# Another order table for a kernel planned by hand: which engine copies and squares, and where a zero-product stands

## The chip, the cores and the metric

The kernel runs on one core of a Trainium2 chip. The metric is the time of one execution in microseconds (us), the median of several runs. A core has a matrix engine (TensorE; PE in the profile, with its weight loads as PEld), a vector engine (VectorE, DVE), a scalar engine (ScalarE, ACT), GpSimd (POOL) and SyncE (SP), which here only issues transfers. Each engine works through its own list of instructions in order; semaphores make one wait for another. SBUF is the working memory, PSUM the eight banks into which PE writes.

## The reference, cut to what matters

```python
# q, k, v: (8, 8, 576, 64); w_in: (512, 1024); w_out: (1024, 512)
kv  = einsum('bhsd,bhse->bhde', k, v)
out = einsum('bhsd,bhde->bhse', q, kv)
x   = out / sqrt(mean(out * out, -1) + 1e-6) * g_norm      # then (4608, 512)
h   = x @ w_in
sm  = softmax(h, -1)
s   = h * sm
ln  = (s - mean(s)) / sqrt(var(s) + 1e-6) * g_ln
y   = ln @ w_out                                            # (4608, 512) float32
```

## The kernel before, in words

There are eight batches, b = 0 to 7. The kernel works in nine chunks c of 512 tokens: chunks 0 to 7 take eight of every nine tokens of a batch, and chunk 8 collects the ninth ones of all batches (`q_last`). Heads come in two halves (`hf`), d_ff in eight slices of 128 (`f`), the tokens of a chunk in four groups (`m`).

Nothing is scheduled by a planner at run time. The source registers named pieces of work, and the text `ORDER` lists all 907 of them; the pieces are emitted in that order, and so each engine's list of instructions is the part of the table that is its own. A suffix (`:act`, `:dve`, `:pool`) sets another engine than the piece's first one. `ROOMS` gives, digit by digit, the buffer of each tile when it is first used (for a PSUM tile one of the eight banks); a piece that takes a buffer waits until the users of the tile that was in it are done. `WARM` says how many products of zeros each `warm` piece has; they only keep PE running.

The pieces, with their lines:

- `k`, `v`, `q`, `q_last`, `w_in`, `w_out` (L322, L338, L343, L348): loads issued by POOL, which convert to bf16 where the tile is bf16. `wide.k` and `wide.v` (L328) bring heads 4 to 7 of batch 0 as float32 on SP's queue, and the pieces `k.0.1` and `v.0.1` copy them to bf16 (L229).
- `kv_mm` (L375): k times v on PE; `kv.b.x.part` (L229): its copies from PSUM.
- `qT_mm` (L427) and its copy `qT.c.hf` (L229): q turned by PE for chunks 0 to 3. For chunks 4 to 8 `qT.c` is one turning transfer on SP's queue (L435).
- `o_mm` (L448): q times kv. `sq` (L233): its squares; `oa` (L460): two halves of them added; `s_mm` (L465): their mean; `ln`, `ex` (L472, L476; chunk 0 by L482): one over the root; `x` (L489): the normalized input of h.
- `h.c.f.part` (L532), in two parts of two matmuls for chunks 0 to 2 and whole afterwards; `exp` (L539) to the tile e; `u` (L543): h times e; `usq` (L233 on ScalarE, L235 on GpSimd): squares of u; `es` (L551, GpSimd): sums of two slices of e.
- `ua`, `usqa`, `esa` (L575): folds of u, its squares and the sums of e on VectorE, for chunks 1 to 8 (esa for 5 to 8).
- `sums` (L594), `turn` (L601), `stats` (L606 to L611), `rstd` (L615, L617): the statistics of the layer norm, `w_mean` (L632) and `w_center` (L638): w_out less its mean.
- `out` (L651; the last group of chunk 8 in two halves, L659), `ob` (L239 on ScalarE, L241 on VectorE): scaled results; `store` (L679, L675).

Three rules tie engines together beside the data. After a fold or an added square on VectorE, the next listed piece of GpSimd waits for it; a turning transfer waits for the last load but one that was issued before it; and a load listed after a turning transfer waits for that:

```python
if engine == "pool":
    self.after(ins, self.adds)
    self.adds.clear()
if name[0] in ("ua", "usqa", "esa", "oa") and engine == "dve":
    self.adds.append(ins)
elif name[0] in ("k", "v", "q", "q_last", "w_in", "w_out") and engine == "pool":
    self.after(ins, self.turns)
...
elif name[0] == "qT" and engine == "sp":
    self.after(ins, self.loads[-2:-1])
    self.turns.append(ins)
```

Of the kernel before, what the change touches and what calls it, by code (L numbers as in the profile page):

```python
# [25 lines left out]
kv.1.0.0.0 kv.1.0.1.1 kv.1.0.1.0 qT_mm.1.0 ex.0.0 q.2.0 qT.1.0:act x.0.0.0 x.0.0.1 warm.5 o_mm.1.0 sq.1.0.0 warm.6
h.0.6.0 h.0.3.0 k.2.0 sq.1.0.1 x.0.1.0 table h.0.0.0 oa.1.0 x.0.1.1 s_mm.1.0 h.0.2.0 h.0.7.0 h.0.2.1 ln.1.0 v.2.0
ex.1.0 h.0.6.1 x.1.0.1 exp.0.6 q.3.0 h.0.3.1 exp.0.2 x.1.0.0 h.0.7.1 h.0.1.0 exp.0.7 u.0.6 v.3.0 qT_mm.1.1 h.0.0.1
exp.0.3 h.0.1.1 u.0.2 usq.0.6 h.1.2.0 exp.0.0 qT.1.1 kv_mm.1.1.1 exp.0.1 kv_mm.1.1.0 k.3.0 kv.1.1.0.1 h.0.4.0 h.0.4.1
u.0.1 kv.1.1.2.1:act kv.1.1.0.0:act es.0.0 kv.1.1.1.0:act kv.1.1.2.0:act kv.1.1.1.1 u.0.3 o_mm.1.1 exp.0.4 h.0.5.0  # L30
# [5 lines left out]
w_center.7 exp.1.4 h.1.5.0 w_center.6 kv.2.1.0:act kv.2.0.0:act h.1.5.1 kv.2.0.2:act kv.2.1.1 kv.2.0.1:act es.1.1  # L36
u.1.4 out.0.2.2 kv.2.1.2:act exp.1.5 o_mm.2.0 u.1.3 o_mm.2.1 sq.2.0.1 out.0.2.3 usq.1.1 u.1.2 qT_mm.3.0 sq.2.0.0 u.1.5
out.0.0.0 sq.2.1.1 oa.2.0 out.0.0.1 sq.2.1.0 qT.3.0 s_mm.2.0 usq.1.5 out.0.0.2 ln.2.0 qT_mm.3.1 oa.2.1:pool ex.2.0
h.1.6.0 qT.3.1 out.0.0.3 usq.1.2:act x.2.0.0 x.2.0.1 h.1.6.1 s_mm.2.1 exp.1.6 sums.0 usq.1.7 ln.2.1 u.1.6 ex.2.1
kv_mm.3.0 es.1.2 turn.0 stats.0 out.0.3.0 kv.3.1.0:act x.2.1.0 x.2.1.1 usq.1.0:act out.0.3.1 usq.1.4 usq.1.3 h.2.6.0  # L40
# [10 lines left out]
exp.3.6 x.4.1.1 h.3.1.0 exp.3.5 q.6.0 usq.2.2:act h.3.4.0 usq.3.3 ob.1.2:act usq.2.1:act usq.2.3:act exp.3.4 es.3.1
u.3.7 u.3.5 store.1.2 h.4.6.0 u.3.6 k.6.0 u.3.4 h.4.7.0 exp.3.1 out.1.1.0 out.1.1.1 exp.4.7 usq.3.2:act h.3.0.0
usqa.2.0 usqa.2.1 exp.4.6 ob.1.1:act u.4.7 kv_mm.5.0 usq.3.5 exp.3.0 u.3.1 sums.2 kv.5.0.1:act es.3.3 h.4.5.0
usq.4.7:act u.4.6 kv.5.0.0:act kv.5.1.2:act h.4.4.0 q.7.0 kv.5.0.2 kv.5.1.1:act u.3.0 kv.5.1.0:act exp.4.5 o_mm.5.1
es.3.0 turn.2 o_mm.5.0 sq.5.1.0 out.2.3.0 stats.2 u.4.5 sq.5.1.1 out.2.3.1 exp.4.4 oa.5.1 ua.3.0 rstd.2 s_mm.5.1
out.2.0.0 ln.5.1 u.4.4 sq.5.0.0 out.2.0.1 sq.5.0.1 ua.3.1 h.4.0.0 ob.2.3:act oa.5.0 ob.2.0 ex.5.1 s_mm.5.0 es.4.2
store.2.3 h.4.2.0 ln.5.0 x.5.1.0 h.4.3.0 store.1.1 usq.3.6 exp.4.2 x.5.1.1 ex.5.0 usq.3.4:act kv_mm.6.0 u.4.2 usq.3.0
qT.6 out.2.1.0 out.2.2.0 kv.6.1.0 kv.6.0.0 es.4.3 kv.6.1.2 x.5.0.0 out.2.2.1 usq.3.7:act qT.7 x.5.0.1 exp.4.3
usq.3.1:act h.4.1.0 es.3.2 kv.6.1.1:act u.4.3 usq.4.5:act kv.6.0.1 ob.2.2:act store.1.0 usqa.3.0 h.5.3.0 exp.4.1
kv.6.0.2:act h.5.6.0 store.2.0 exp.5.3 exp.4.0 usqa.3.1 u.4.1 h.5.7.0 es.4.0 es.4.1 usq.4.6:act u.4.0 out.2.1.1  # L60
exp.5.6 u.5.3 exp.5.7 o_mm.6.0 ob.2.1 o_mm.6.1 sq.6.0.0 sums.3 u.5.6 store.2.1 out.3.0.0 sq.6.0.1 u.5.7 usq.4.2:act
oa.6.0 out.3.0.1 sq.6.1.1 ua.4.0 sq.6.1.0 s_mm.6.0 out.3.3.0 ln.6.0 oa.6.1 turn.3 out.3.3.1 ex.6.0 v.7.0 stats.3
q_last.3 s_mm.6.1 x.6.0.0 h.5.0.0 ln.6.1 k.7.0 x.6.0.1 h.5.2.0 ex.6.1 q_last.1 exp.5.0 x.6.1.0 h.5.5.0 q_last.7
exp.5.2 u.5.0 h.5.4.0 rstd.3 es.5.1 x.6.1.1 usq.4.4:act out.3.1.0 ob.3.0 exp.5.4 es.5.3 h.6.6.0 usq.4.3:act ob.3.3
usq.4.0:act u.5.4 h.6.3.0 exp.5.5 ua.4.1 h.5.1.0 usq.4.1:act u.5.5 q_last.0 exp.6.6 out.3.1.1 u.5.2 q_last.4
# [670 lines left out]
```

## Time and profile before

| | |
|---|---|
| median of three runs | 177.41 us (176.84 to 177.65) |
| span of the profiled execution, first to last instruction | 175.8 us |
| what lies around it, against that median | 1.6 us |
| PE busy | 164.2 us |
| ScalarE busy | 152.1 us |
| VectorE busy | 145.5 us |
| GpSimd busy | 99.8 us |
| granted clock of PE | 1.000 |

A row of the timeline gives the start in us, the duration in us, engine, line, operation, output and input tiles with their shape, how many instructions were merged (x), and in brackets the idle time of the engine before it and what ended it. Durations of neighbours overlap a little, because one instruction ends its writes while the next begins; the interval from start to start is the price in a full queue. Rows of groups give the mean in ns after the sum. SPq and POOLq are the queues' own times.

### The profile page before, as it was taken

To read this page: it belongs to the slowest core of one execution; us is meant where nothing else is said; L and a number is where in the kernel's file an instruction comes from. 1 tells how busy PE (TensorE), PEld (TensorE's weight loads), DVE (VectorE), ACT (ScalarE), POOL (GpSimd) and SP (SyncE) were. 2 spreads that over 40 slices of the span, in tenths; PEclk is the share of its full clock that TensorE was granted. 3 is DMA by queue.
4 is the path that set the end of the run, shared out by engine and by line. 5 is a ranking of instruction groups with operands and counts; after the bars stand their busy time and mean duration, and the time that the engine had idled before them with its cause. 6 is when DMAs were issued, how large, how long until landed. Compare 5 with 4: busy or idle time off the path is not lost.

```text
span 175.8 us, 4843 instructions
## 1 busy us (share of the span) xinstructions
PE 164.2 (93%) x1913; PEld 80.3 (46%) x1938; DVE 145.5 (83%) x317; ACT 152.1 (86%) x273; POOL 99.8 (57%) x108
## 2 busy tenths in 40 slices
...
GB/s 179 218 203 214 206 275 373 209 208 208 208 210 210 218 210 129 127 206 235 205 183 259 150 52 193 156 73 93 195 206 105 5 118 126 2 60 93 196 213 159
DMA packets 34623, 30.27 MB, mean 172 GB/s; under 512 B 16288, under 2 KB 28328, under 8 KB 34600
## 3 DMA queue, kind: packets, MB, share of 16 engines
...
q8 instruction: 15, 0.25, 0.6%
q14 instruction: 8, 0.07, 0.1%
HBM read 32.51 MB, written 9.44 MB: 239 GB/s over the span
## 4 chain that ended last, share of the span: by engine, by line
PE 75%; DVE 10%; ACT 5%; DMA 5%; issue 2%; POOL 1%; POOLq 0%; DVEq 0%; ACTq 0%
PE h_ps L532 31%; PE out_ps L651 30%; DMA k_sb<-in_k_dram 5%; PE kv_ps L375 4%; PE o_ps L448 3%; DVE u_sb L543 3%; PE sum_ps L594 3%; PE s_ps L465 3%; DVE x_sb L489 2%; DVE w_out_sb L638 2%; ACT osq_sb L233 2%; DVE osq_sb L460 1%; PE out_ps L659 1%; ACT e_sb L539 1%; ACT kvd L229 1%
## 5 line engine op out<-in xcount | busy, mean ns | idle before, releaser
L532 PE MATMUL h_ps<-x_sb,w_in_sb 128*128 128x512 bf16 x280 | 68.0, 379 | 0.5
L651 PE MATMUL out_ps<-w_out_sb,u_sb 128*128 128x512 bf16 x266 | 65.2, 379 | 0.7 <-issue 0.3
L551 POOL TENSOR_TENSOR es_sb<-e_sb 128x512 bf16<-128x512 f32 x36 | 45.4, 1279 | 33.5 <-ACT e_sb L539 13.0
L539 ACT ACTIVATE e_sb<-h_ps,zero_t 128x512 f32<-128x512 f32 x72 | 46.2, 690 | 2.3 <-PE h_ps L532 1.7
L543 DVE TENSOR_TENSOR u_sb<-h_ps,e_sb 128x512 bf16<-128x512 f32 x72 | 46.6, 684 | 1.3 <-ACT e_sb L539 1.0
L532 PEld LDWEIGHTS <-w_in_sb 128*128 128x128 bf16 x288 | 27.3, 98 | 32.5 <-issue 1.3
L651 PEld LDWEIGHTS <-u_sb 128*128 128x128 bf16 x280 | 26.4, 98 | 31.6 <-issue 1.0
L233 ACT ACTIVATE usq_sb<-u_sb,zero_t 128x512 bf16<-128x512 bf16 x49 | 33.6, 718 | 0.0
L489 DVE SCALAR_TENSOR_TENSOR x_sb<-o_ps,g_sb,rst_sb 128x256 bf16<-128x256 f32 x72 | 30.2, 478 | 3.1 <-ACT rst_sb L476 2.5
L235 POOL TENSOR_TENSOR usq_sb<-u_sb 128x512 bf16<-128x512 bf16 x23 | 23.6, 1043 | 7.9 <-DVE osq_sb L460 5.6
L233 ACT ACTIVATE osq_sb<-o_ps,zero_t 128x512 bf16<-128x512 f32 x36 | 22.8, 689 | 3.5 <-PE o_ps L448 3.4
L239 ACT ACTIVATE ob_sb<-out_ps,rstd 128x512 f32<-128x512 f32 x22 | 14.8, 684 | 4.0 <-PE out_ps L651 3.8
L575 DVE TENSOR_TENSOR usq_sb<-usq_sb 128x2048 bf16<-128x2048 bf16 (+2 forms) x20 | 17.0, 848 | 0.6 <-ACT usq_sb L233 0.4
L229 DVE CAST kvd<-kv_ps 64x128 bf16<-64x128 f32 (+3 forms) x26 | 6.4, 256 | 11.2 <-ACT kvd L229 6.5
L241 DVE TENSOR_SCALAR ob_sb<-out_ps,rstd 128x512 f32<-128x512 f32 (+1 forms) x15 | 10.6, 711 | 4.1 <-PE out_ps L659 2.2
L322 POOL DMA_DIRECT2D v_sb<-in_v_dram x9 | 6.8, 757 | 10.1 <-DVE sum_ps L601 2.8
L472 ACT ACTIVATE lss_sb<-s_ps,eps_t 128x512 f32<-128x512 f32 x16 | 11.1, 695 | 1.0 <-PE s_ps L465 0.7
L476 ACT ACTIVATE rst_sb<-lss_sb,zero_t 128x512 f32<-128x512 f32 x16 | 11.5, 722 | 0.4
L375 PE MATMUL kv_ps<-v_sb,k_sb 64*64 64x64 bf16 x576 | 8.0, 194 | 2.8 <-DMA k_sb<-in_k_dram 1.3
L300 PE MATMUL warm_ps<-zeros 128*128 128x512 bf16 x25 | 8.8, 481 | 1.4 <-DVE zeros L255 1.2
L229 ACT CAST kvd<-kv_ps 64x128 bf16<-64x128 f32 (+3 forms) x34 | 8.2, 243 | 2.2 <-PE kv_ps L375 1.5
L375 PEld LDWEIGHTS <-k_sb 64*64 64x64 bf16 x576 | 6.8, 107 | 6.8 <-DMA k_sb<-in_k_dram 2.6
...
## 6 DMA issues: line engine op xcount, KB each, us to landing
...
k_sb<-in_k_dram POOLq DMA_DIRECT2D x6, 576.0 KB, 13.8
...
```

What stands on the lines that cost most here:

```text
L229: nc.scalar.copy(dst, src) if engine == "act" else on[engine].tensor_copy(dst, src)
L233: nc.scalar.activation(out=dst, in_=src, func=AF.Square, bias=zero_t[:, :])
L235: on[engine].tensor_tensor(out=dst, in0=src, in1=src, op=MUL)
L239: nc.scalar.activation(out=dst, in_=src, func=AF.Copy, scale=by)
L375: nc.tensor.matmul(t[64 * y:64 * y + 64, :], T["k", b][rows, n, i, :], T["v", b][rows, n, i, :], start=(i == 0 and (b < 2 or m == 0)), sto ...
L489: nc.vector.scalar_tensor_tensor(out=t[:, 2 * hf + dh, z], in0=T["o", c, hf, z][:, dh], scalar=g_rep[dh], in1=T["rst", c, hf][:, z], op0=M ...
L532: nc.tensor.matmul(bank(("h", c, f), [128, 512])[:, :], w_in_sb[:, dt, f * 128:(f + 1) * 128], T["x", c][:, dt].rearrange("p a b c -> p (a ...
L539: nc.scalar.activation(out=t[:, f % 2, :], in_=T["h", c, f][:, :], func=AF.Exp, bias=zero_t[:, :])
L543: nc.vector.tensor_tensor(out=t[:, f, :], in0=T["h", c, f][:, :], in1=T["e", c, f // 2][:, f % 2, :], op=MUL)
L551: on[engine].tensor_tensor(out=t[:, n, :], in0=e[:, 0, :], in1=e[:, 1, :], op=ADD)
L575: nc.vector.tensor_tensor(out=to[:, 0:n, :], in0=src[:, 0:n, :], in1=src[:, n:2 * n, :], op=ADD)
L651: nc.tensor.matmul(bank(("out", c, m), [128, d_model])[:, :], T["u", c][:, f, m * 128:(m + 1) * 128], w_out_sb[:, f, :], start=(f == 0), s ...
```

## The change

Only three tables change; no piece is added or taken out (907 before and after).

- `ORDER`: another order throughout. The start takes heads 0 to 3 of batch 0 first (`v.0.0 k.0.0 q.0.0 q.0.1 q.1.0 v.1.0 k.1.0 w_in.0 w_in.1`) where it took 4 to 7 first (`q.0.1 v.0.0 k.0.0 q.0.0 ... v.1.0 k.1.0 q.1.0 w_in.0 ... w_in.1`).
- Engines: 42 of the 72 squares of u are on ScalarE and 30 on GpSimd (49 and 23 before). `k.0.1` goes from ScalarE to VectorE. `oa.7.0` goes to GpSimd and `oa.2.1` comes back to VectorE. Of the copies of kv and qT and of the scaled results other ones are on ScalarE and VectorE, as many on each as before.
- `WARM`: 29 2 3 1 3 3 1 for 14 3 1 3 1 4 1, so 42 zero-products for 27; `warm.6` stands in the middle of the w_mean pieces, no longer ahead of the first h.
- `ROOMS`: other buffers.

The diff, cut to the stretches that the text speaks of:

```diff
 ORDER = """
-wide.v ident wide.k g_rows q.0.1 v.0.0 k.0.0 q.0.0 v.0.1:act v.1.0 k.1.0 q.1.0 w_in.0 k.0.1:act w_in.1 warm.0
...
-u.0.5 es.0.2 w_mean.1 w_mean.2 w_mean.3 w_mean.4 w_mean.5 w_mean.6 usq.0.5:act x.1.1.1 usq.0.2 usq.0.7:act w_mean.7
-x.1.1.0 usq.0.0 q.4.0 usq.0.4:act w_center.5 h.1.3.0 qT_mm.2.1 h.1.7.0 w_center.1 h.1.4.0 h.1.7.1 qT.2.1:act q.5.0
-w_center.4 h.1.0.1 v.4.0 w_center.0 exp.1.7 qT_mm.2.0 exp.1.0 w_center.3 h.1.1.0 h.1.1.1 k.4.0 qT.2.0:act w_center.2
-h.1.2.1 es.0.1 u.1.7 h.1.3.1 exp.1.1 h.1.4.1 u.1.0 exp.1.3 out.0.2.0 es.1.0 usq.0.3 u.1.1 exp.1.2 out.0.2.1 kv_mm.2.0
...
-usqa.1.0 kv.3.0.2:act h.2.4.0 exp.2.6 h.2.5.0 ob.0.3:act ua.1.0 o_mm.3.0 h.2.1.0 store.0.3 sq.3.0.0 h.2.0.1 sq.3.0.1
-u.2.6 h.2.1.1 store.0.0 exp.2.0 h.2.5.1 usqa.1.1 out.0.1.0 exp.2.1 oa.3.0 h.2.4.1 ua.1.1 exp.2.5 qT.4 s_mm.3.0
...
-rstd.1 x.3.1.1 usq.2.0 o_mm.4.0 o_mm.4.1 ob.1.3 sq.4.0.1 out.1.0.0 usq.2.4 x.3.1.0 sq.4.0.0 store.1.3 out.1.2.1
...
+ident v.0.0 k.0.0 q.0.0 q.0.1 q.1.0 warm.0 kv_mm.0.0.0 kv_mm.0.0.1 kv.0.0.0.0 wide.k kv.0.0.2.0 kv.0.0.1.1 k.0.1
+kv.0.0.2.1 v.1.0 k.1.0 w_in.0 w_in.1 warm.1 qT_mm.0.0 qT.0.0 q.1.1 warm.2 qT_mm.0.1 kv.0.0.0.1:act wide.v v.0.1:act
...
+u.0.7 sq.1.1.1 sq.1.1.0 oa.1.1 s_mm.1.1 exp.0.0 k.3.0 v.3.0 exp.0.1 u.0.0 ln.1.1 w_mean.2 warm.6 h.1.1.0 u.0.5 w_mean.3
+w_mean.4 w_mean.5 h.1.0.0 w_mean.6 w_mean.7 u.0.1 ex.1.1 x.1.1.0 x.1.1.1 w_center.3 w_center.2 w_center.0 h.1.3.0
...
+h.1.2.1 usq.1.4 k.4.0 kv_mm.2.0 kv.2.1.2 kv.2.1.0 u.1.3 kv.2.0.2:act kv.2.1.1:act kv.2.0.1:act kv.2.0.0:act out.0.0.0
+out.0.2.2 usq.0.0 exp.1.2 o_mm.2.0 sq.2.0.0 sq.2.0.1 u.1.5 u.1.2 qT.4 usq.1.7 o_mm.2.1 out.0.0.1 sq.2.1.0 sq.2.1.1
+usq.0.7 qT_mm.3.0 out.0.0.2 oa.2.0 s_mm.2.0 ln.2.0 qT.3.0 ex.2.0 out.0.0.3 out.0.2.3 oa.2.1 s_mm.2.1 ln.2.1 usq.1.1
+usq.1.3:act es.1.0 ex.2.1 es.1.2 x.2.0.1 sums.0 turn.0 usq.1.2:act h.1.6.0 stats.0 qT.5 x.2.0.0 out.0.3.0 out.0.3.1
...
+usq.1.5:act out.0.3.3 kv.3.1.0:act kv.3.1.1:act ob.0.3:act kv.3.0.1 store.0.2 store.0.3 store.0.0 kv.3.1.2:act
...
+out.1.2.1 ob.1.3 x.3.1.1 sq.4.0.1 sq.4.0.0 es.2.1 v.5.0 oa.4.0 sq.4.1.1 sq.4.1.0 oa.4.1 out.1.0.0 out.1.0.1 ob.1.2:act
+store.1.2 q_last.4 q.7.0 ua.2.0 s_mm.4.0 ln.4.0 ex.4.0 ob.1.0 h.3.7.0 x.4.0.1 x.4.0.0 h.3.0.0 es.2.0 h.3.5.0 h.3.3.0
...
+out.8.1.0 out.8.0.0 out.8.0.1 stats.8 rstd.8 ob.8.2 ob.8.0 store.8.2:act store.8.0 out.8.1.1 ob.8.1 store.8.1 out.8.3.1
+ob.8.3.1 out.8.3.0 store.8.3.1:act ob.8.3.0:act store.8.3.0:act
 """
 WARM = """
-14 3 1 3 1 4 1
+29 2 3 1 3 3 1
 """
```

In `ROOMS`, the scaled result `ob.1.3` has the buffer that `ob.0.2` had (before: the one of `ob.0.3`), `warm.6` and then h.1.2 the bank of h.0.0, and `h.1.1` the bank of `s_mm.1.1`.

124 lines of the change are left out of this document (59 added, 65 removed).

## The prediction

> **What bounds the kernel now.** I read the page's busy times and the shares of its chain first, then one table of windows cut at the places that matter here, then the matrix engine's timeline.
>
> ```profile
> PE 164.2 (93%) x1913; PEld 80.3 (46%) x1938; DVE 145.5 (83%) x317; ACT 152.1 (86%) x273; POOL 99.8 (57%) x108
> PE 75%; DVE 10%; ACT 5%; DMA 5%; issue 2%; POOL 1%; POOLq 0%; DVEq 0%; ACTq 0%
> 19.84:26.60 6.76, 6.62 (x36) 2.92 (x36) 4.57 (x12) 6.66 (x11) 3.16 (x5) 1.00 1.18 253
> 26.60:47.86 21.26, 19.23 (x251) 10.37 (x254) 19.52 (x36) 19.51 (x38) 19.01 (x19) 1.00 1.23 240
> 47.86:91.00 43.14, 42.72 (x684) 21.02 (x690) 41.35 (x89) 41.66 (x80) 27.81 (x28) 1.00 1.08 194
> 91.00:172.57 81.57, 80.80 (x744) 38.62 (x750) 73.09 (x151) 73.04 (x129) 38.19 (x36) 1.00 0.65 130
> ```
>
> In the windows the columns are the length, then busy PE, PEld, DVE, ACT and POOL, then clock, DMA share and GB/s. From 47.86 us to the last matmul PE idles 0.42 + 0.77 = 1.2 us of 124.7. An order table cannot remove matmuls, so it can win only in three places: before 19.84, where h starts; between 26.60 and 47.86, where PE idles 2.0 us; and in those 1.2 us. From 47.86 to 91 VectorE (41.35) and ScalarE (41.66 of 43.14) are nearly as full as PE, so there a late step of either shows at once.
>
> ```profile
> 10.10 0.70 POOL L322 DMA_DIRECT2D q_sb<-in_q_dram  x1 [1.14 <-DMA v_sb<-in_v_dram]
> 17.39 0.45 PEld L427 LDWEIGHTS <-q_sb 128*128 128x128 bf16 x8 [0.82 <-DMA q_sb<-in_q_dram]
> 19.83 0.98 PEld L532 LDWEIGHTS <-w_in_sb 128*128 128x128 bf16 x6 [0.27 <-DMA w_in_sb<-in_moe_w_in_dram]
> 26.60 0.65 PEld L375 LDWEIGHTS <-k_sb 64*64 64x64 bf16 x36 [0.42 <-DMA k_sb<-in_k_dram]
> 31.08 0.38 PE L465 MATMUL s_ps<-osq_sb,head_mean 128*128 128x512 bf16 x1 [0.71 <-DVE osq_sb L460]
> 31.10 1.95 PE L632 MATMUL mean_ps<-u_sb,ua_sb 128*128 128x512 f32 x7
> 34.08 0.62 PE L427 MATMUL qt_ps<-ident,q_sb 128*128 128x128 bf16 x8 [0.57 <-DMA q_sb<-in_q_dram]
> 34.53 1.89 PE L532 MATMUL h_ps<-x_sb,w_in_sb 128*128 128x512 bf16 x7
> 40.40 0.77 PE L375 MATMUL kv_ps<-v_sb,k_sb 64*64 64x64 bf16 x72 [0.51 <-DVE u_sb L543]
> 41.10 1.04 PE L532 MATMUL h_ps<-x_sb,w_in_sb 128*128 128x512 bf16 x3
> 47.86 0.63 PE L594 MATMUL sum_ps<-u_sb,stat_sel 128*32 128x128 bf16 x32
> 70.19 7.07 PE L532 MATMUL h_ps<-x_sb,w_in_sb 128*128 128x512 bf16 x32
> 98.14 0.64 PE L448 MATMUL o_ps<-qT_sb,kvd 64*32 64x256 bf16 x32
> 98.71 0.29 PE L594 MATMUL sum_ps<-ua_sb,stat_sel 128*32 128x128 bf16 x8
> ```
>
> Taken from one start to the next, these rows give PE's prices: 0.216 a matmul of 512 columns ((7.07 - 0.17 of drain)/32), 0.45 a qT_mm, 0.70 a kv_mm, 0.29 an o_mm (0.57/2), 0.25 a w_mean. The bracketed waits of 0.71, 0.57 and 0.51 are 1.8 of the 2.0 idle.
>
> **The start: 0.** Heads 0 to 3 come first instead of 4 to 7, but the same seven small loads stand ahead of w_in.0 and w_in.1 on POOL's queue, and h starts on w_in.0 (19.84). The new first step waits for k.0.0, the queue's second load; before, the second, v.0.0, was in by 10.1. From there: kv_mm.0.0 to 10.9; copies of kv and k.0.1's cast to 12.2; the copy qT.0.0 to 12.9; kv_mm.0.1.0 and o_mm.0.0 to 13.8; two squares to 15.1; s_mm.0.0, behind turn_g, qT_mm.1.0 and warm.3, to 16.1; ex.0.0 to 16.8. That is early, since k.1.0, now seventh, comes when the seventh, q.1.0, came: 17.4. Then kv_mm.1.0 to 18.1, three copies to 18.8, x.0.0.0 to 19.7, just under w_in.0. Both tables put the same steps before h and the same thirteen half-parts of h before kv_mm.1.1, which waits for k.1.1: both are at 26.60. The longer warm.0 (29 matmuls for 14) covers the wait for k.0.0. If that margin of 0.15 fails, up to 0.5 is lost.
>
> ```profile
> 6.31 1.15 ACT L229 CAST k_sb<-u_sb 128x1152 bf16<-128x1152 f32 x1 [0.23 <-DMA u_sb<-in_k_dram]
> 15.33 0.69 DVE L293 TENSOR_SCALAR ua_sb<-g_sb 128x1024 fp32r<-128x1024 f32 x1
> 23.67 3.58 ACT L539 ACTIVATE e_sb<-h_ps,zero_t 128x512 f32<-128x512 f32 x6
> 32.84 1.93 ACT L233 ACTIVATE usq_sb<-u_sb,zero_t 128x512 bf16<-128x512 bf16 x3
> 34.73 1.01 ACT L229 COPY qT_sb<-qt_ps 128x1024 bf16<-128x1024 bf16 x1
> 41.26 1.28 ACT L229 CAST kvd<-kv_ps 128x128 bf16<-128x128 f32 x5 [0.68 <-PE kv_ps L375]
> 42.04 2.48 DVE L543 TENSOR_TENSOR u_sb<-h_ps,e_sb 128x512 bf16<-128x512 f32 x4
> L235 POOL TENSOR_TENSOR usq_sb<-u_sb 128x512 bf16<-128x512 bf16 x23 | 23.6, 1043 | 7.9 <-DVE osq_sb L460 5.6
> ```
>
> The copy k.0.1 goes from ScalarE (1.15) to VectorE: 0.78 by the f32 row of 1024 columns scaled to 1152, 1.15 at most. It ends before q.0.0's turn is copied; 0, with 0.3 as the far bound.
>
> **From 26.60 to sums.0: -0.5.** Before, this takes 21.26. The work in it is 19 half-parts of h and 8 quarter-parts of out, 2 matmuls each (11.6), three s_mm (0.65), four qT_mm (1.8), two kv_mm (1.4), three o_mm (0.9), eight w_mean (2.0): 18.3, so 2.9 is lost. The new table has two half-parts and one qT_mm fewer ahead of sums.0: 17.0. Its losses I get by walking the table, giving each step its interval (exp 0.58, u 0.60, square 0.60 to 0.62, copy of kv 0.21 to 0.27, of qT 1.01) behind the last of its sources. What goes: q.2.0's wait (0.57), as its turn stands behind seven half-parts of h, at 36.7; the wait for u before kv_mm.2.0 (0.51), as some u stand between the w_centers. What comes: o_mm.1.1 waits for four copies of kv on VectorE (0.28); warm.6 takes h.0.0's bank and waits for u.0.0 (0.38, and 0.22 itself); h.1.1.0 waits for ln.1.1's bank (0.25); out.0.2.0 for the copy qT.2.0 (0.17); o_mm.2.0 and .1 for the copies of kv.2, four on ScalarE behind exp.1.3 (0.63); s_mm.2.0 and 2.1 for their added squares (0.34), s_mm.1.1 likewise (0.10); hand-offs 0.1. Sum 2.45, 0.5 less. Bounds: none of the new waits, -2.9; each half as long again, +0.7. POOL issues k.3.0 and v.3.0 behind three sums of e, about 4 later. The queue's backlog hides it (the DMA share stays at 1.23 through the window); kv_mm.3.0 needs them at 49.6.
>
> **ScalarE's seven squares: -0.4.** They go to GpSimd: 7 x 0.60 = 4.2 off ScalarE, 7 x 1.04 = 7.3 on POOL, which was busy 27.8 of 43.1 after 47.86. Swaps of kv, qT and ob copies keep their numbers on each engine; oa.7.0 goes to POOL and oa.2.1 comes back. This buys time only where PE waits for ScalarE:
>
> ```profile
> 82.94 0.83 PE o_ps L448 x32
> 90.35 0.84 PE kv_ps L375 x72
> ```
>
> Against 0.57 and 0.70 these two rows of the chain lose 0.4, and I take that; bounds 0 and -1.2 (all of PE's idle time).
>
> **The stores on SP's queue: +0.6.** Before, store.0.3 and store.0.0 stand ahead of the turns qT.4 and qT.5, and ob.1.3 writes into the buffer of store.0.3. In the new table both turns come first, and ob.1.3 takes the buffer of store.0.2, the first store behind them.
>
> ```profile
> 54.52 2.46 SPq L679 DMA_DIRECT2D out_dram<-ob_sb  x4
> 57.18 6.24 SPq L435 DMA_TRANSPOSE qT_sb<-q_sb  x2
> 63.53 4.47 SPq L679 DMA_DIRECT2D out_dram<-ob_sb  x6
> DMA to landing us min/median/max: 2.3/3.7/4.5
> 66.18 0.68 DVE ob_sb L241
> ```
>
> The landing times are of the stores between 50 and 70 us. The turns can start once q.4.0 is there, 56.0 to 57.2 (no earlier stores occupy SP); they hold the queue for 6.24, so store.0.2's second half goes out at 62.8 to 64.0 and lands, with the median, at 66.6 to 67.7, middle 67.1. VectorE reaches ob.1.3 at 66.18 before, some 65.8 after. It waits 1.3; x.3.1.1, oa.4.0, oa.4.1 and ua.2.0 are queued behind, and s_mm.4.0 waits for oa.4.0. PE has out.1.0 to do meanwhile, so I charge it 0.6. Bounds: 0 (lands at 65.1) and 2.2 (lands at 68.5).
>
> **Folds and the end: 0.** Added squares and folds on VectorE read two operands from SBUF, as GpSimd's sums do.
>
> ```profile
> 28.21 2.52 POOL L551 TENSOR_TENSOR es_sb<-e_sb 128x512 bf16<-128x512 f32 x2
> 30.23 0.79 DVE L460 TENSOR_TENSOR osq_sb<-osq_sb 128x512 bf16<-128x512 bf16 x1
> L460 DVE TENSOR_TENSOR osq_sb<-osq_sb x15: 414/423/790, 20.9 to 136.5; 128x512 bf16<-128x512 bf16 x15
> 170.83 0.69 ACT L239 ACTIVATE ob_sb<-out_ps,rstd 128x512 f32<-128x512 f32 x1 [1.21 <-PE out_ps L651]
> 172.57 0.48 DVE L241 TENSOR_SCALAR ob_sb<-out_ps,rstd 128x256 f32<-128x256 f32 x1 [0.39 <-PE out_ps L659]
> ```
>
> One of fifteen took 0.79 for 0.42, and it ran into a sum on POOL that ended at 30.73. So a fold that starts inside a GpSimd step is held until its end: at most 1.04 for a square. POOL steps listed behind a fold wait for it (the code's rule), so only a late POOL collides; I take 0, bounds 0 and 7 x 1.04. The Trainium skill, SBUF — State Buffer, section "Who interferes with whom", says that a VectorE instruction with two SBUF inputs contends with a GpSimd instruction that reads SBUF, and that the later one is blocked. By that rule the trace agrees (0.79 against 0.42); it speaks against seven more squares on GpSimd, and by it alone the sum would be the third rival's. The last scaling moves to ScalarE: between 0.48 and the 0.69 of twice the columns, 0 to +0.2; I take 0.
>
> **Sum.** 0 - 0.5 - 0.4 + 0.6 + 0 = -0.3 on the profiled span of 175.8. The median of the runs, 177.41, stands 1.6 above that span; with the same 1.6, 175.5 + 1.6 = 177.1.
>
> **Rivals.**
> First, more is won: half of the waits that I add in the early stretch do not arise (-1.2), because those steps are not as late as my walk makes them, and the rest holds: 175.9. For it: the table interleaves u and w_center; against it: VectorE and ScalarE are 92% busy there, so a late step is the rule.
> Second, slower, by one mechanism: the store behind the turns. If store.0.2 lands at the maximum, 68.5, PE pays 2.2 instead of 0.6: 178.7. It decides from a landing at 68.2 (a price of 1.9). For it: the DMA share of 1.08 between 48 and 91, so stores land among loads; against it: k.4.0 is the last load before the turns, so the backlog ends there, and 4.5 is the largest landing of ten.
> Third, folds held by GpSimd: two held for a whole square between 48 and 91, where VectorE has 1.8 free of 43.1, cost 2.1 less that slack's half: +1.2, 178.3.
> Fourth, the change does nothing here: what ScalarE gains is hidden behind PE and the early waits only change place: 177.4.
>
> **How the numbers follow.** A measurement of this kernel tells about 0.5%, 0.9 us, from no change. Chances: the forecast 0.42 (own range 176.3 to 178.0), more won 0.27, the store 0.16, the folds 0.08, nothing 0.07. Faster by over 0.5% (under 176.5): 0.25 of the forecast's and nine tenths of the first rival's, 0.36. Slower (over 178.3): most of the second, half of the third, a little of the forecast's, 0.22. Within: 0.42. The range takes in the first rival with 0.5 below it and the second: 175.4 to 178.7.
>
> **What would show it.** Right: h starts at 19.8 to 20.4 and kv_mm.1.1 at 26.6 to 27; sums.0 starts at about 46.1 with PE's largest waits at o_mm.2.0 and warm.6; ob.1.3 on VectorE waits for a store at 65 to 67; ScalarE's busy time is 5 lower and POOL's 7 higher; PE is 98% busy from 48. Wrong: a start of h after 20.6; idle time of PE over 2.5 between 48 and 172; additions on VectorE often far above 0.42, which would be the third rival; no wait at ob.1.3, which takes away my +0.6.

## The result, and the profile after

The new table is slower: 183.31 us, median of four runs (182.27 to 183.58), against 177.22 (176.84 to 177.65) for the kernel before on the same chip. The ratio is 1.0321 (95% interval 1.0279 to 1.0363). The forecast was 177.1, with a range of 175.4 to 178.7. The profiled execution took 183.51 us, its span is 181.7 at a granted clock of 0.996, so that 1.8 lies around it.

The first two lines are of the page of the changed kernel: busy times, and the shares of its chain.

```profile
PE 168.7 (93%) x1929; PEld 81.8 (45%) x1953; DVE 148.4 (82%) x318; ACT 146.1 (80%) x265; POOL 107.3 (59%) x115
PE 37%; DMA 19%; ACT 16%; DVE 10%; issue 8%; POOL 5%; SPq 3%; ACTq 0%; POOLq 0%
```

ScalarE is 6.0 lower and GpSimd 7.5 higher, as forecast. But only 37% of the chain is PE (75% before); transfers have 19% and ScalarE 16%. Of PE's 4.5 us more of busy time 3.2 are the fifteen added zero-products (L299, 0.216 each); the rest wasn't taken apart.

Windows of the changed kernel, cut at h, `kv_mm.1.1`, `sums.0`, `sums.1`, `sums.2` (length, then busy PE, PEld, DVE, ACT, POOL, then clock, DMA share, GB/s):

```profile
20.57:27.15 6.58, 6.44 (x35) 3.08 (x35) 4.59 (x11) 6.47 (x10) 4.55 (x7) 1.00 1.16 242
27.15:48.14 20.99, 18.73 (x239) 9.33 (x243) 18.48 (x35) 17.59 (x33) 16.96 (x18) 1.00 1.22 234
48.14:63.91 15.77, 15.47 (x317) 8.14 (x319) 14.95 (x32) 15.59 (x29) 9.47 (x9) 1.00 1.20 186
63.91:89.00 25.09, 22.24 (x260) 10.07 (x255) 21.64 (x46) 20.69 (x40) 17.85 (x19) 1.00 1.04 190
89.00:178.28 89.28, 88.31 (x874) 41.89 (x876) 80.44 (x162) 77.12 (x140) 48.52 (x46) 1.00 0.65 127
```

The same cut of the kernel before behind `sums.0`:

```profile
47.86:61.47 13.61, 13.50 (x234) 6.63 (x235) 13.42 (x30) 13.13 (x26) 7.97 (x8) 1.00 1.21 212
61.47:80.48 19.01, 18.80 (x281) 9.31 (x283) 18.21 (x40) 18.26 (x34) 13.11 (x14) 1.00 0.96 174
80.48:172.57 92.09, 91.21 (x917) 43.70 (x920) 82.81 (x172) 83.31 (x151) 44.92 (x42) 1.00 0.71 138
```

Between `sums.1` and `sums.2` PE idles 2.85 of 25.09 us, where it idled 0.21 of 19.01. The tables put different steps into these stretches, so lengths alone can't be compared. I take a lag: the start of a `sums`, less the time of all matmuls listed ahead of it, from the first `kv_mm` on, at the prediction's prices (a `sums` of chunks 1 to 4 at 0.56). A lag that grows is time lost. Ahead of `sums.0` stand 30.08 us of work before and 28.77 after, ahead of `sums.1` 43.22 and 43.92, ahead of `sums.2` 61.94 and 65.10, ahead of `sums.8` 146.89 in both. The starts, first of the kernel before, then of the changed one:

```profile
61.47 0.29 PE L594 MATMUL sum_ps<-ua_sb,stat_sel 128*32 128x128 bf16 x8
80.48 0.30 PE L594 MATMUL sum_ps<-ua_sb,stat_sel 128*32 128x128 bf16 x8
```

```profile
63.91 0.30 PE L593 MATMUL sum_ps<-ua_sb,stat_sel 128*32 128x128 bf16 x8
89.00 0.30 PE L593 MATMUL sum_ps<-ua_sb,stat_sel 128*32 128x128 bf16 x8
```

At `sums.1` the lag is 63.91 - 43.92 = 19.99 against 61.47 - 43.22 = 18.25, so 1.74 lost by then; at `sums.2` it is 23.90 against 18.54, 5.36 lost. This table gives what each kernel lost in each stage of its profiled execution against the profiled execution of the kernel before, with the ratio of its runs. The last stage ends at the start of `sums.8`. Negative is a gain.

| kernel | to h | h to sums.0 | to sums.1 | to sums.2 | to the end | sum | ratio (95%) |
|---|---|---|---|---|---|---|---|
| changed | 0.73 | 0.86 | 0.15 | 3.61 | 0.40 | 5.75 | 1.032 (1.028 to 1.036) |
| e1 first stores ahead of turns | 1.24 | 0.80 | 0.15 | 3.26 | 0.86 | 6.31 | 1.033 (1.028 to 1.039) |
| e2 copies by bank | 0.89 | 0.70 | 0.18 | 2.68 | 0.39 | 4.84 | 1.021 (1.015 to 1.027) |
| e3 w_out early | 0.83 | 0.86 | 0.23 | 3.82 | 0.08 | 5.82 | 1.030 (1.026 to 1.035) |
| e4 = e1 + e2 + e3 | 1.39 | 0.70 | 0.15 | 1.61 | 0.31 | 4.16 | 1.021 (1.018 to 1.025) |
| e5 = e4 + later stores | 0.82 | 0.67 | 0.14 | 0.81 | 0.01 | 2.45 | 1.016 (1.014 to 1.019) |
| e6 = e5 + early edits | -0.04 | 0.41 | 0.14 | 1.33 | 0.46 | 2.30 | 1.017 (1.015 to 1.019) |
| e9 = e6 + squares back | 0.09 | 0.42 | 0.15 | 1.25 | 3.18 | 5.09 | 1.032 (1.029 to 1.035) |
| e12 all stores alone | 0.75 | 0.79 | 0.14 | 4.03 | 0.07 | 5.78 | 1.028 (1.025 to 1.031) |
| e7 old table, squares | -0.47 | -0.10 | -0.01 | 0.01 | 1.56 | 0.99 | 1.009 (1.007 to 1.010) |
| e8 old table, turns first | 0.14 | -0.19 | -0.01 | 0.02 | -0.01 | -0.05 | 1.000 (0.998 to 1.001) |
| e10 old table, copies late | -0.47 | 0.14 | -0.01 | 0.58 | 0.09 | 0.33 | 1.003 (1.001 to 1.005) |
| e11 old table, three moves | 0.67 | -0.15 | 0.00 | 0.01 | 0.11 | 0.64 | 0.999 (0.998 to 1.001) |

Its grain: a stage that an edit doesn't touch repeats within 0.2 in most rows, but the start of h does not. In five profiles with the old start it lies between 19.37 and 20.51 (mean 19.81). A profiled execution can lie up to 1.5 us above the median of its kernel (e2 and e12 do), so the stages are those of one execution each. The ratios leave one disturbed run of e2 and one of e12 out.

Where the 3.61 goes is read from four lists of the changed kernel. ScalarE, then PE, SyncE's queue and GpSimd's loads:

```profile
66.58 0.27 ACT L228 CAST kvd<-kv_ps 128x128 bf16<-128x128 f32 x1 [1.67 <-DVE kvd L228]
73.45 0.69 ACT L238 ACTIVATE ob_sb<-out_ps,rstd 128x512 f32<-128x512 f32 x1 [1.44 <-DMA out_dram<-ob_sb]
68.21 0.70 PE L447 MATMUL o_ps<-qT_sb,kvd 64*32 64x256 bf16 x32 [0.76 <-DVE u_sb L542]
74.19 1.89 PE L531 MATMUL h_ps<-x_sb,w_in_sb 128*128 128x512 bf16 x8 [1.03 <-ACT ob_sb L238]
76.44 1.04 PE L531 MATMUL h_ps<-x_sb,w_in_sb 128*128 128x512 bf16 x4 [0.36 <-DVE x_sb L488]
57.32 5.81 SPq L434 DMA_TRANSPOSE qT_sb<-q_sb  x2
63.17 16.59 SPq L678 DMA_DIRECT2D out_dram<-ob_sb  x14
66.38 0.80 POOL L321 DMA_DIRECT2D k_sb<-in_k_dram  x1
68.73 0.78 POOL L321 DMA_DIRECT2D v_sb<-in_v_dram  x1
```

First, `kv.4.0.0` on ScalarE waits 1.67 for `kv.4.0.2` on VectorE, which copies out of the same bank and is listed behind `turn.1` and `stats.1`; `exp.2.2`, `u.2.2` and `o_mm.4.0` follow late. Second, `ob.1.2` waits 1.44 for `store.0.0`, the last of six halves behind the turns, with `ln.4.0` and `ex.4.0` queued behind it. The next experiments ask which of the two counts.

### The profile page after: what moved, and what is told of

Read it like the earlier page. It is cut to its first block, busy times and chain, and to the rows that moved or that the text cites. A ratio compares the mean times of both kernels' runs of the same rounds, so it can differ in the third digit from the quotient of the medians.

```text
span 181.7 us, 4899 instructions
## 1 busy us (share of the span) xinstructions
PE 168.7 (93%) x1929; PEld 81.8 (45%) x1953; DVE 148.4 (82%) x318; ACT 146.1 (80%) x265; POOL 107.3 (59%) x115
## 4 chain that ended last, share of the span: by engine, by line
PE 37%; DMA 19%; ACT 16%; DVE 10%; issue 8%; POOL 5%; SPq 3%; ACTq 0%; POOLq 0%
PE out_ps L650 16%; PE h_ps L531 16%; DMA out_dram<-ob_sb 11%; DMA q_sb<-in_q_dram 5%; ACT ob_sb L238 4%; DMA u_sb<-in_moe_w_out_dram 4%; DVE u_sb L542 4%; ACT e_sb L538 3%; SPq L678 3%; ACT usq_sb L232 2%; ACT osq_sb L232 2%; DVE w_out_sb L637 2%; ACT kvd L228 1%; PE sum_ps L593 1%; POOL q_sb L321 1%
## 5 line engine op out<-in xcount | busy, mean ns | idle before, releaser
L531 PE MATMUL h_ps<-x_sb,w_in_sb 128*128 128x512 bf16 x279 | 68.7, 379 | 2.2 <-ACT ob_sb L238 1.0
L650 PE MATMUL out_ps<-w_out_sb,u_sb 128*128 128x512 bf16 x268 | 65.9, 379 | 1.2 <-DVE x_sb L488 0.3
L234 POOL TENSOR_TENSOR usq_sb<-u_sb 128x512 bf16<-128x512 bf16 x30 | 30.9, 1041 | 11.1 <-DVE osq_sb L459 8.5
L232 ACT ACTIVATE usq_sb<-u_sb,zero_t 128x512 bf16<-128x512 bf16 x42 | 29.0, 716 | 0.8 <-DVE u_sb L542 0.8
L238 ACT ACTIVATE ob_sb<-out_ps,rstd 128x512 f32<-128x512 f32 (+1 forms) x22 | 14.7, 676 | 7.7 <-PE out_ps L658 3.8
L228 DVE CAST kvd<-kv_ps 64x64 bf16<-64x64 f32 (+3 forms) x26 | 6.5, 251 | 11.4 <-PE kv_ps L374 10.7
L299 PE MATMUL warm_ps<-zeros 128*128 128x512 bf16 x41 | 12.5, 452 | 1.6 <-DVE zeros L254 1.2
L574 DVE TENSOR_TENSOR ua_sb<-u_sb 128x2048 bf16<-128x2048 bf16 x8 | 10.8, 1349 | 0.1
L447 PE MATMUL o_ps<-qT_sb,kvd 64*32 64x256 bf16 (+1 forms) x384 | 7.2, 246 | 3.4 <-ACT kvd L228 1.8
L337 POOL DMA_DIRECT2D q_last<-in_q_dram x8 | 6.1, 765 | 5.8 <-DVE osq_sb L459 5.8
```

The source lines that it names most:

```text
L228: nc.scalar.copy(dst, src) if engine == "act" else on[engine].tensor_copy(dst, src)
L232: nc.scalar.activation(out=dst, in_=src, func=AF.Square, bias=zero_t[:, :])
L234: on[engine].tensor_tensor(out=dst, in0=src, in1=src, op=MUL)
L238: nc.scalar.activation(out=dst, in_=src, func=AF.Copy, scale=by)
L299: nc.tensor.matmul(t[:, :], zeros[:, 0:128], zeros[:, :], start=True, stop=True)
L531: nc.tensor.matmul(bank(("h", c, f), [128, 512])[:, :], w_in_sb[:, dt, f * 128:(f + 1) * 128], T["x", c][:, dt].rearrange("p a b c -> p (a ...
```

## The experiments

No edit changes the buffer of any tile. The experiments ran on several chips, each against the kernel before on the same chip, so kernels are compared by their ratios rather than by their times.

**e1, the stores ahead of the turns.** SyncE's part of the table:

```diff
-qT.4 qT.5 store.0.2 store.0.3 store.0.0 store.1.2 store.1.0 store.0.1 store.1.3
+store.0.2 store.0.3 store.0.0 qT.4 qT.5 store.1.2 store.1.0 store.0.1 store.1.3
```

> The changed kernel (183.3 us) with one edit: on SyncE's queue the stores store.0.2, store.0.3 and store.0.0 stand ahead of the two turns qT.4 and qT.5, as in the kernel before; nothing else moves. Theory S (the stores behind the turns): in the changed kernel the last half of store.0.0 goes out at 66.9, lands at 73.4, and ob.1.2 on ScalarE waits 1.4 for it, with ln.4.0 and ex.4.0 behind it and PE idle 1.03 and 0.36 for what follows. The stores now go out before 60 and land before 66, the wait of 1.4 is gone, and the run takes about 181.8 (-1.5). Rival C (the copies): the stretch from 64 to 75 is set by ScalarE's copies of kv.4, which wait 1.67 for VectorE; those stay, so that less than 0.4 is won: 183.0. Rival L: the store lands late because of the loads beside it, wherever it stands: 183.3.

Measured: 183.76 us, nothing won (0.35 in the stretch from `sums.1` to `sums.2`). SyncE, GpSimd and ScalarE of e1:

```profile
58.79 6.07 SPq L434 DMA_TRANSPOSE qT_sb<-q_sb  x2
69.15 0.81 POOL L321 DMA_DIRECT2D k_sb<-in_k_dram  x1 [2.27 <-PE o_ps L447]
84.86 0.69 ACT L238 ACTIVATE ob_sb<-out_ps,rstd 128x512 f32<-128x512 f32 x1 [0.93 <-DMA out_dram<-ob_sb]
```

The wait at `ob.1.2` is gone, but ten us later `ob.1.1` waits 0.93 for `store.1.3`, and the turns, now 1.5 later, push the load `k.5.0` from 66.38 to 69.15. (The row names PE for that wait; but the table lists the load behind the turns, and it follows the last landing event of the second turn, at 68.59, by 0.56.) Theory S alone falls; so does L in its words, since the store did land in time. Rival C's size fits: the copy's wait of 1.67 is still there. The wait for a store came back in another place.

**e2, one bank's copies to one engine.**

```diff
-kv.1.0.1.0:act kv.1.0.0.0:act kv.1.0.0.1 kv.1.0.2.1 kv.1.1.0.1:act kv.1.1.2.0 kv.1.1.1.0
+kv.1.0.1.0 kv.1.0.0.0 kv.1.0.0.1:act kv.1.0.2.1:act kv.1.1.0.1 kv.1.1.2.0:act kv.1.1.1.0:act
...
-kv.2.1.1:act kv.4.0.2 kv.4.1.2:act
+kv.2.1.1 kv.4.0.2:act kv.4.1.2
```

> The changed kernel with the copies of kv sorted by PSUM bank for kv.1.0, kv.1.1, kv.2 and kv.4: the three copies out of one bank go to one engine (ten suffixes change; VectorE and ScalarE keep their numbers but for one copy more on VectorE at kv.2). Theory C: two engines that copy out of one bank wait for each other in the listed order, and this costs 0.66 ahead of h (o_mm.1.0), 0.3 at o_mm.1.1, 0.5 at o_mm.2.0 and 0.6 at o_mm.4.0. h then starts at 19.9 instead of 20.57, no ScalarE copy waits for a VectorE copy, sums.0 comes about 1.3 earlier (46.8), and the run takes about 181.4 (-1.9). Rival S (the store sets the stretch from 64 to 75): what is won at o_mm.4.0 is lost again at ob.1.2, which waits for the same landing: 182.0 (-1.3 from the early part). Rival N: the copies are late for another reason, the engines being busy, and sorting only moves the wait: 183.3.

Measured: ratio 1.021, some 1.9 us won over the changed kernel, of which the stages of the one profiled execution show 0.9 between `sums.1` and `sums.2` and 0.16 ahead of `sums.0`. The wait at `o_mm.4.0` is gone. The early waits only shrink: `o_mm.1.0` from 0.66 to 0.40, `o_mm.1.1` from 0.51 to 0.28, `o_mm.2.0` from 0.82 to 0.73, and h did not come earlier (20.73). ScalarE now reaches `ob.1.2` early and waits longer:

```profile
72.55 0.69 ACT L238 ACTIVATE ob_sb<-out_ps,rstd 128x512 f32<-128x512 f32 x1 [2.07 <-DMA out_dram<-ob_sb]
```

So C holds for `kv.4` and only in small part for the early copies, and S's sentence about it holds too: part of what is won at `o_mm.4.0` is lost at the store.

**e3, w_out ahead of the added square.**

```diff
-oa.1.0 ... w_out.0 exp.0.2 w_out.1 ... q.2.0
+w_out.0 w_out.1 q.2.0 oa.1.0 ... exp.0.2 ...
```

> The changed kernel with the loads w_out.0, w_out.1 and q.2.0 listed ahead of the added square oa.1.0, as in the kernel before, so that GpSimd's queue doesn't wait for it from 12.9 to 22.6. Theory W: the loads behind that wait are up to 8 late, w_out lands at 29.5 to 31, w_mean and w_center come late, VectorE's eight w_centers push u and the copies of kv.2 back, and about 1.0 of the 1.6 lost by sums.0 comes from it: sums.0 at about 47.1, the run 182.3 (-1.0). Rival C: the waits at o_mm.1.1 (0.51) and o_mm.2.0 (0.82) come from the copies alone and the late loads are hidden: 183.3.

Measured: 182.87 us, intervals overlapping those of the changed kernel; from h to `sums.0` it loses 0.86, as without the edit. GpSimd's wait of 9.7 us, which the prediction had not seen, was hidden.

**e4, all three.**

> The three edits together: stores ahead of the turns, copies of kv sorted by bank, w_out and q.2.0 ahead of oa.1.0. If the three causes are the whole loss and add up (1.5 + 1.9 + 0.3 to 1.0), the run takes 178.5 to 179.6. If the loss lies in the stage's balance (seven squares on GpSimd, folds held by GpSimd, sums late), it stays above 181.5. Below 177.2 it would beat the kernel before, which would mean that the new table's other moves are a gain of at least 1.

Measured: 181.39 us, above the sum of the parts (178.5 to 179.6), below the 181.5 of the other theory by too little to tell. Between `sums.1` and `sums.2` it loses 1.61; one store is still waited for:

```profile
83.26 0.69 ACT L238 ACTIVATE ob_sb<-out_ps,rstd 128x512 f32<-128x512 f32 x1 [0.83 <-DMA out_dram<-ob_sb]
```

**e5, the later stores too.** Against e4, again SyncE's part:

```diff
-qT.4 qT.5 store.1.2 store.1.0 store.0.1 store.1.3
+qT.4 qT.5 store.0.1 store.1.3 store.1.2 store.1.0
```

> The kernel of the three edits (181.4 us) with one more: store.0.1 and store.1.3 are listed right behind ob.0.1 and ob.1.3, so that on SyncE's queue they stand ahead of store.1.2 and store.1.0. Theory S: what ScalarE's ob.1.1 waits for at 83.3 (0.83; PE idle 0.73 behind it) is store.1.3, the last of eight halves that the queue sends from 71.6 on because store.1.2 in front of them waits for ob.1.2. Now store.1.3 goes out at about 70, lands before 78, the wait is gone, and with PE's 0.73 and its restart 0.9 is won: 180.5. Rival: ScalarE or VectorE is late there anyway, so that 0.3 at most is won: 181.1.

Measured: 180.27 us, ratio 1.016. Against e4's 1.021 that is 0.8 us, and the intervals overlap; but the stage from `sums.1` to `sums.2` shows the same 0.8 (1.61 to 0.81), and no `ob` waits for a store there. Theory S is right for this store.

**e6, two edits ahead of sums.0.** Against e5:

```diff
-kv.0.0.0.0 wide.k kv.0.0.2.0 kv.0.0.1.1 k.0.1 ... kv.0.0.0.1:act wide.v v.0.1:act
+wide.k k.0.1 wide.v v.0.1:act kv.0.0.0.0 kv.0.0.2.0 kv.0.0.1.1 ... kv.0.0.0.1:act
...
-usq.0.2 q.5.0 es.0.0
+es.0.0 usq.0.2 q.5.0
```

> The kernel before this one in the list (e5) with two edits in the early part: GpSimd's sum es.0.0 goes ahead of usq.0.2 and the load q.5.0, and the casts v.0.1 (ScalarE) and k.0.1 (VectorE) go ahead of the copies of kv.0.0. Theory B (VectorE, ScalarE and GpSimd wait for each other): ScalarE's wait of 1.9 for es at 36.4 goes, the exps, u and the copies of kv.2 come earlier, PE's wait at o_mm.2.0 (0.74) goes, and sums.0 comes 0.6 earlier after h; the cast v.0.1 no longer waits for VectorE's copies until 12.5, kv_mm.0.1 starts at 12.9 instead of 13.7 and h 0.5 earlier. Together 1.1 less than e5: 179.4 if e5 is at 180.5. Rival D: h waits for k.1.0's landing (17.4) and w_in.0 (19.8), so the casts bring 0.2 at most, and the wait at o_mm.2.0 is VectorE's eight w_centers, which no sum on GpSimd moves: 0.3 less than e5.

What it undoes, in the changed kernel: a cast on ScalarE queued behind a copy that waits for VectorE, and an exp that waits for GpSimd's sum.

```profile
12.40 0.21 ACT L228 CAST kvd<-kv_ps 128x64 bf16<-128x64 f32 x1 [10.37 <-DVE kvd L228]
12.51 1.15 ACT L228 CAST v_sb<-u_sb 128x1152 bf16<-128x1152 f32 x1
13.71 0.47 PE L374 MATMUL kv_ps<-v_sb,k_sb 64*64 64x64 bf16 x18 [0.71 <-ACT v_sb L228]
20.57 1.89 PE L531 MATMUL h_ps<-x_sb,w_in_sb 128*128 128x512 bf16 x8
36.43 0.69 ACT L538 ACTIVATE e_sb<-h_ps,zero_t 128x512 f32<-128x512 f32 x1 [1.94 <-POOL es_sb L550]
44.37 0.65 PE L447 MATMUL o_ps<-qT_sb,kvd 64*32 64x256 bf16 x32 [0.82 <-ACT kvd L228]
```

In e6:

```profile
13.06 0.47 PE L374 MATMUL kv_ps<-v_sb,k_sb 64*64 64x64 bf16 x18
19.80 1.46 PE L531 MATMUL h_ps<-x_sb,w_in_sb 128*128 128x512 bf16 x6
43.16 0.65 PE L447 MATMUL o_ps<-qT_sb,kvd 64*32 64x256 bf16 x31 [0.74 <-DVE kvd L228]
66.39 0.80 POOL L321 DMA_DIRECT2D k_sb<-in_k_dram  x1 [1.20 <-DMA qT_sb<-q_sb]
77.56 0.77 PE L374 MATMUL kv_ps<-v_sb,k_sb 64*64 64x64 bf16 x72 [0.20 <-DMA v_sb<-in_v_dram]
```

Theory B is right up to `sums.0`: `kv_mm.0.1.0` starts 0.65 earlier, h at 19.80 (20.57 to 21.23 in the seven profiles of the new table without these two edits, mean 20.8; 19.93 in e9, which has the edit too), and `sums.0` is 1.1 earlier than in e5. Not in one point: the wait at `o_mm.2.0` stays. And the time is 180.42, not less than e5's 180.27. The 1.1 are given back: 0.5 from `sums.1` to `sums.2`, 0.45 behind. In the first of these `k.5.0` now waits 1.20 for the turns and is issued at 66.39, hardly ahead of e5's 66.59. PE then waits 0.20 for `v.5.0`, which is less than half of the 0.5; 0.26 behind VectorE and 0.17 behind ScalarE come to it, which e5 doesn't have. What gives back the second half was not taken apart.

**e7, the squares alone, on the old table.**

```diff
-usq.4.4:act usq.4.5:act usq.4.6:act usq.5.2:act usq.5.5:act usq.6.0:act usq.6.4:act
+usq.4.4 usq.4.5 usq.4.6 usq.5.2 usq.5.5 usq.6.0 usq.6.4
```

> The kernel before the change (177.2) with seven squares moved from ScalarE to GpSimd and nothing else: usq.4.4, 4.5, 4.6, 5.2, 5.5, 6.0, 6.4. The prediction's step: ScalarE gets 4.2 free, PE's waits for ScalarE's copies (0.4) go, 176.8. Rival F: the squares delay GpSimd's sums and loads and collide with VectorE's folds, each hit costing up to 1.04: 178 to 179. Rival H: PE doesn't wait for either there: 177.2.

Measured: ratio 1.0085, slower by 1.5 us; all of it arises behind `sums.2`. VectorE, GpSimd and ScalarE of e7:

```profile
108.57 1.47 DVE L575 TENSOR_TENSOR ua_sb<-ua_sb 128x1024 bf16<-128x1024 bf16 x1
108.17 1.30 POOL L551 TENSOR_TENSOR es_sb<-e_sb 128x512 bf16<-128x512 f32 x1
113.77 1.04 POOL L235 TENSOR_TENSOR usq_sb<-u_sb 128x512 bf16<-128x512 bf16 x1 [1.89 <-DVE usq_sb L575]
116.07 1.26 ACT L539 ACTIVATE e_sb<-h_ps,zero_t 128x512 f32<-128x512 f32 x2 [2.35 <-POOL es_sb L551]
```

A square that has come to GpSimd stands at 113.77 where a sum of e stood; the sum follows it at 114.78, and ScalarE, which the move was to relieve, waits 2.35 for the buffer of e. And folds are held: this one takes 1.47 for the 0.68 of its kind, begun 0.4 into a sum that ends at 109.47; two more behind `sums.2` take 1.32 for 0.68 and 1.54 for 1.22, so 1.7 in all on VectorE. By the Trainium skill, SBUF — State Buffer, section "Who interferes with whom", the later of two such instructions is blocked; the trace agrees. Rival F is right. The longest wait comes through the sums; how the 1.5 divides between late sums and held folds isn't shown.

**e8, the turns first, on the old table.**

```diff
-store.0.3 store.0.0 qT.4 qT.5 store.0.1 store.0.2 store.1.3
+qT.4 qT.5 store.0.3 store.0.0 store.0.1 store.0.2 store.1.3
```

> The kernel before the change (177.2) with the turns qT.4 and qT.5 ahead of store.0.3 and store.0.0 on SyncE's queue and nothing else. The prediction's step put 0.6 on this (0 to 2.2): ob.1.3 writes into the buffer of store.0.3, which now goes out behind the turns at about 62 and lands at 65 to 68; ob.1.3 is reached at 66.2. So 177.8. Rival: the landing takes 5.9 as in the changed kernel, ob.1.3 or ob.1.0 waits over 2, and PE loses 1.5: 178.7. Rival: the stores land in time because only two stand there: 177.2.

Measured: ratio 0.9995 (0.998 to 1.001): nothing. VectorE's `ob.1.3` of e8 waits for nothing, and its stores' median landing (last number, us) in the window 55 to 75 is 2.4; in the changed kernel, from 60 to 76, it is 4.8 (in each view seven of ten stores have a landing on record).

```profile
66.07 0.75 DVE L241 TENSOR_SCALAR ob_sb<-out_ps,rstd 128x512 f32<-128x512 f32 x1
69.70 0.81 POOL L322 DMA_DIRECT2D v_sb<-in_v_dram  x1 [2.64 <-DVE osq_sb L460]
```

The row of the DMA issues of e8, then of the changed kernel:

```profile
out_dram<-ob_sb SPq DMA_DIRECT2D x10, 128.0 KB, 2.4
```

```profile
out_dram<-ob_sb SPq DMA_DIRECT2D x10, 128.0 KB, 4.8
```

The stores behind the turns are harmless by themselves. In e8 the loads of chunk 5 follow at 69.7, behind the stores; in the new table they go out at 66.4 and 68.7, among them. The landing events of the changed kernel show the same split: the first four halves behind the turns took 2.5 to 3.7, the fifth and the sixth, beside the load of 66.38, took 6.0 and 5.9.

**e9, the squares back on ScalarE, on e6.** The seven suffixes of e7, `:act` added.

> The kernel e6 (180.4 us) with the seven squares usq.4.4, 4.5, 4.6, 5.2, 5.5, 6.0 and 6.4 back on ScalarE, each at its place in the list. Theory F (a square on GpSimd makes its sums of e late, and ScalarE's exps wait for the buffers of e; the old kernel with these squares moved lost 1.4 between sums.3 and sums.5): 0.9 comes back between sums.3 and sums.4, 179.4. Rival G: the new table was built round them, ScalarE is 95% busy from 90 to 115 and gets 4.2 more, so that it becomes the bound: 181 to 182. Rival H: neither; PE's waits there (0.28, 0.28) are hand-offs: 180.4.

Measured: 183.36 us, ratio 1.032 against e6's 1.017, so 2.6 worse, all of it behind `sums.2`. The stretch from `sums.2` to `sums.6`, of e6 and then of e9:

```profile
85.49:149.24 63.75, 63.21 (x718) 29.70 (x710) 58.01 (x120) 58.10 (x106) 39.29 (x39) 1.00 0.71 127
```

```profile
85.56:152.03 66.47, 64.47 (x717) 29.88 (x710) 58.71 (x120) 62.06 (x113) 32.51 (x32) 1.00 0.68 122
```

ScalarE has 4.0 more to do and the stretch is 2.7 longer, with ScalarE busy for 62.06 of 66.47. Rival G has the sign right, with too small a size (181 to 182). The same seven squares cost 1.5 when they go to GpSimd in the old table and 2.6 when they go back in the new one: their price is set by what is listed round them.

**e10, the copies of kv.4 late and split, on the old table.**

```diff
-turn.1 es.2.2 out.1.3.0 kv.4.1.0 kv.4.0.1:act ... kv.4.0.0 ... stats.1 out.1.2.0 kv.4.0.2:act kv.4.1.1
+turn.1 stats.1 kv.4.0.2 es.2.2 out.1.3.0 kv.4.1.0 kv.4.0.1:act ... out.1.2.0 kv.4.1.1 kv.4.1.2 kv.4.0.0:act
```

> The kernel before the change (177.4) with the one pattern of the new table that e2 undid: VectorE does stats.1 straight behind turn.1 and only then its copies of kv.4, and one bank's copies are split (kv.4.0.2 on VectorE ahead of kv.4.0.1 and kv.4.0.0 on ScalarE; each engine keeps its number). Theory C: ScalarE's first copy, which runs at 63.4, waits for VectorE's at 64.3, with ln.3.1, ex.3.1 and the squares of o.4 behind it; x.3.1 and ob.1.3 are 0.9 later, and PE, which has out.1.0 and out.1.2 to do, loses 0.5 to 0.9 at o_mm.4 and s_mm.4: 178.1. Rival: the slack in out.1 covers it, 177.4. Rival: copies out of one bank on two engines don't wait for each other at all, and ScalarE's copy starts at 63.4 as before: 177.4, and ScalarE shows no wait.

Measured: ratio 1.0031 (1.001 to 1.005), 0.5 us slower; the stage from `sums.1` to `sums.2` loses 0.58. ScalarE of e10 now has a wait that the kernel before has not:

```profile
63.80 0.26 ACT L229 CAST kvd<-kv_ps 64x128 bf16<-64x128 f32 x1 [0.74 <-DVE kvd L229]
```

In this program copies out of one bank on two engines run one after the other, in listed order. The kernel before splits this bank too, but lists ScalarE's copy first; what e10 adds is a VectorE copy that is late and stands ahead of it. The Trainium skill, PSUM — Partial Sum Buffer, section "PSUM bank collisions raise a hardware error", says that two engines reading the same part of a bank (a quarter of its partitions) at once collide and that the hardware doesn't hold them apart, so the program must. No run here let two reads meet. The wait above is stricter than that page asks: `kv.4.0.1` and `kv.4.0.2` read different halves of the partitions, and the one still waits for the other. C is right, at the lower end of its range.

**e11, three moves on PE's list, on the old table.**

```diff
-s_mm.1.1 ... w_mean.1 w_mean.2 w_mean.3
+w_mean.1 w_mean.2 w_mean.3 s_mm.1.1 ...
...
-qT_mm.2.1 h.1.7.0 h.1.4.0 h.1.7.1 ... kv_mm.2.0 ... out.0.2.2
+h.1.7.0 h.1.4.0 h.1.7.1 qT_mm.2.1 ... out.0.2.2 kv_mm.2.0 ...
```

> The kernel before the change (177.4) with three moves on TensorE's list alone, into its three early waits: w_mean.1 to 3 ahead of s_mm.1.1 (wait 0.71), qT_mm.2.1 three half-parts of h later (0.57), out.0.2.2 ahead of kv_mm.2.0 (0.51). Theory D: from 50 on, loads and turns pace the kernel (in e6 1.1 won by sums.0 was given back by sums.4, with k.5.0's load behind the turns and kv_mm.5.0 waiting for v.5.0); so sums.0 comes 1.2 to 1.6 earlier, and half or more of it is given back: 176.6 to 177.2. Rival: PE is the bound, so that all of it stays: 175.9, faster than both kernels. Rival: the steps moved later make ScalarE and VectorE late: 177.6 or more.

Measured: ratio 0.9993. All three waits are gone, but from h to `sums.0` only 0.15 is won: PE waits elsewhere.

```profile
34.55 1.16 PE L532 MATMUL h_ps<-x_sb,w_in_sb 128*128 128x512 bf16 x4 [0.64 <-DVE x_sb L489]
37.26 2.32 PE L532 MATMUL h_ps<-x_sb,w_in_sb 128*128 128x512 bf16 x10 [0.22 <-ACT qT_sb L229]
```

None of the three is right as told: nothing was given back after `sums.0`, because little had been won. PE's idle time ahead of `sums.0` is not PE's to win; VectorE and ScalarE, 92% busy there, hand out the work.

**e12, all stores, no copies.** The edits of e1 and e5 on the changed kernel.

> The changed kernel (183.3 us) with both edits of SyncE's queue and none of the copies: store.0.2, store.0.3 and store.0.0 ahead of the turns, store.0.1 and store.1.3 ahead of store.1.2 and store.1.0. It closes the square for the stretch from sums.1 to sums.2, in which the changed kernel loses 3.6 against the kernel before, sorting the copies alone 2.7, moving the first three stores alone 3.3, and copies and all stores together 0.8. Theory M (one wait stands behind the other on ScalarE, so that each covers the other): with every wait for a store gone the copies' wait of 1.67 is left with its 1.0 to 1.3 at PE, the stretch loses 1.8 to 2.1, and the run takes about 181.6 to 182. Rival A (they add up): 3.6 less 1.9 (0.8 against 2.7) leaves 1.7: 181.4; the two differ little here, and what tells them apart from the third is the size. Rival S (the stores alone set it): under 1.0 is lost, 180.7.

Measured: ratio 1.028 (1.025 to 1.031), five runs from 181.91 to 183.51 us, median 182.06. By the median that is the upper end of theory M; by the ratio it is 0.7 less than the changed kernel, with intervals that overlap. The profiled execution is the longest of the five. In it no store is waited for from 60 to 90, yet the stretch loses 4.03. GpSimd, PE and SyncE's queue of e12:

```profile
69.70 0.80 POOL L321 DMA_DIRECT2D k_sb<-in_k_dram  x1 [3.34 <-DMA qT_sb<-q_sb]
81.44 0.77 PE L374 MATMUL kv_ps<-v_sb,k_sb 64*64 64x64 bf16 x72 [1.60 <-DMA v_sb<-in_v_dram]
57.71 7.73 SPq L434 DMA_TRANSPOSE qT_sb<-q_sb  x2
```

A third wait was behind the other two. The turns, behind the stores, end later; `k.5.0` is listed behind them and waits 3.34; `v.5.0` follows it; `kv_mm.5.0` waits 1.60. In e4 and e5, which have the same turns, `k.5.0` goes out at 67.08 and 66.59. The landing events show a part of the difference. A turn has sixteen of them, and in e1, e4, e5 and e12 the load follows the last one by 0.56 or 0.57. In e12 and e1 the sixteenth comes 1.5 behind the fifteenth (69.14 after 67.61, 68.59 after 67.06); in e4 and e5 it comes with it (66.51, 66.03). What holds it back isn't shown, and with one profile each it could be an accident of those executions. Whether the earlier loads of e3's edit make the turns end sooner was not tried by itself.

## Why the prediction was wrong, by its steps

**The start, 0: wrong by 0.7 to 1.0.** The walk has `k.0.1`'s cast on VectorE and leaves out `v.0.1`'s, which stands on ScalarE's list behind a copy that waits for five steps of VectorE. The margin of 0.15 was gone before `k.1.0` landed; e6 gives 0.9 of it back.

**From 26.60 to sums.0, -0.5: wrong; +1.0** (0.55 late at `kv_mm.1.1`, 1.59 at `sums.0`). The places were right: `o_mm.1.1` 0.51 (forecast 0.28), `o_mm.2.0` 0.82 (0.63), `warm.6` 0.22 (0.38), `s_mm.2.0` 0.22. The sizes were not, as one bank's copies wait for each other, and so was the premise that the old waits are won when they go: e11 takes them away and wins 0.15.

**ScalarE's squares, -0.4: wrong in sign.** The work came off ScalarE, as told, yet the stages behind `sums.2` lose 0.4. On the old table alone the move costs 1.5 (e7); inside the new table taking it back costs 2.6 (e9), so the move has no price of its own. The step asked where PE waits for ScalarE, not what on GpSimd is listed behind the square and who waits for that.

**The stores behind the turns, +0.6 (0 to 2.2): a step of this stage failed, with the largest miss.** The time in the queue was right (`store.0.2`'s second half at 63.81; forecast 62.8 to 64.0). But it lands at 66.35, sooner than forecast, and `ob.1.3` does not wait; it comes at 70.0, behind late copies. `ob.1.2`, which I passed over, waits for `store.0.0`, the sixth half, which takes 5.9 to land where I took 3.7 with 4.5 as the largest. That maximum came from the old kernel, whose loads don't stand there, and from six stores: four of the ten in that view have no landing on record. And the step priced one wait by itself. The stretch has three, stores, copies and the loads behind the turns, that cover each other: in the profiled executions single edits bring 0.4 (e1), 0.9 (e2) and, for all stores, less than nothing (e12), all together 2.8 of 3.6 (e5).

**The copies of kv, "keep their numbers": the step that was missing.** I counted copies for each engine and passed over the listed order of two engines on one bank. By e2 this is a third of the loss by the ratios (1.032 to 1.021) and a sixth by the two profiles (0.9 of 5.75).

**Folds and end, 0: right in size.** From the last matmul to the end of the span it is 0.2 more than before; one fold of eight of its form is held (2.25 for 1.22), at 166.3.

**The rivals.** The first and the fourth did not come true. The second, the store behind the turns, had the right sign and the right queue, with 178.7 for a price of 2.2; it was priced as one landing and not as a chain. The third came true only in e7. What would show the forecast wrong was named rightly: h after 20.6 nearly (20.57), PE idle over 2.5 from 48 on (it is 4.1), no wait at `ob.1.3`.

**What stays open.** e5 and e6, the best versions of the new table, are 1.6% slower than the kernel before. Of e5's 2.45, 0.8 lies ahead of h and goes with e6's casts; 0.7 lies between h and `sums.0` and 0.8 in the stretch with the turns, and their causes are not shown. Nor is shown why e6's early gain is lost again behind `sums.2`. No version beat the kernel before.
